# The first chunk's first two attention-times-V blocks issued together, and the next chunk's normalising at other units

## The chip, the cores and the metric

The kernel runs on one core of a Trainium2 chip, in one launch. The metric is the device time of an execution in microseconds (us), the median of several executions. Before the change it is 556.62 us, the median of 3 runs (556.55 to 556.70).

## The reference, cut to what matters

Everything is bfloat16; S = 2048 positions, D = 576, F = 4608, 32 heads of 18.

```python
xn  = layernorm(x)                                  # rows of 576
q, k, v = split(xn @ wqkv)                          # 32 heads of 18
s   = where(0 <= i - j < 256, q k^T / sqrt(18), -1e9)
att = softmax(s) @ v                                # then @ wo
out = x + att @ wo + (silu(xn @ w1) * (xn @ w3)) @ w2
```

## The kernel before, in words

**Tiling.** The 2048 positions are cut into four chunks of 512 (`NC`, `CH`); a chunk is four x tiles of 128 rows. Each chunk has three stages: the projections for q, k and v; then 36 units, each of which makes 128 of the 4608 columns of the gated hidden layer and leaves them in `hT`; then the second stage, which multiplies `hT` by w2 and the attention's output `oT` by wo and writes the result. For chunk 0 the layernorm of its four x tiles and its projections come before the loop over chunks.

**A unit.** It is 18 matmuls in 9 pairs (`unit_pairs`, L746): every matmul uses 64 rows of the array, and the two of a pair go to the two row halves at once, one into each of two PSUM banks. Then ScalarE (ACT) takes the tanh of one bank (`unit_tanh`, L755), and VectorE (DVE) makes `gs` from that bank (L761) and `hT` from `gs` and the other bank (L764). Only when that second DVE instruction has read its bank may TensorE (PE) write the pair of banks again.

**Banks.** Six of the eight PSUM banks are three pairs (`JOBS`), which `job()` deals out in turn: unit u uses the pair that unit u-3 used. The last two banks (`SC`) hold scores. An attention-times-V block takes pairs from the same turn.

**Attention.** The 32 heads are 8 groups of four. In chunk 0 a group has four score steps, 32 in all. A step is 4 or 6 small matmuls on PE (`scores`, L612), an exponential on ACT (`exps`, L621), and one or two masking multiplications on GpSimd (POOL, `masks`, L649). Blocks `pv(c, j)` (L676) multiply the probabilities of groups 2j and 2j+1 by V: 72 matmuls on a 64x20 tile each in chunk 0, 96 in the later chunks. The first matmul of a block waits for the masks of all its steps, and the first one into each bank waits for that bank's last reader. DVE then transposes the two result banks (`pv_out`, L693) and takes reciprocals (L697); POOL scales (`o_scale`, L702); DVE transposes back (`o_turn`, L709); DMAs pack the result into `oT` (`o_pack`, L734).

**Order.** The program is written out by a planner in one pass, and each engine runs its own part strictly in that order, with semaphores where an operand comes from another engine. Between the pairs of the units the planner places score steps by a counter (`clock`, one per pair): the first when it reaches `START`, later ones spaced so that they end before the chunk's last unit, with `PV_COST` counters set aside for every block to come. `BLOCKS` says which blocks are issued together, `AT` in front of which pair of which unit the first of them goes, and `HOLD` keeps score steps away from that place. In chunk 0 before the change blocks 0, 1 and 2 are issued one by one, each at the end of a unit; in chunks 1 to 3 blocks 0 and 1 go together in front of pair 6, 7 or 8 of unit 18, and two probability buffers serve as room for the two extra transposes. Block 3 comes in the second stage in all chunks.

**The next chunk's normalising.** While a chunk's units run, the x tiles of the next chunk are loaded by SyncE's DMA queue (SP; `load_x`, L298; in chunk 0 at units 11, 13, 15 and 17). At the end of the unit that `near` names for a tile, behind that unit's two DVE instructions, DVE takes the statistics (L388 twice, L391), and POOL the inverse root (L370, L372); at a later named unit DVE applies them (L406 twice), and at another a transposing DMA on SP (L448) sends the result to `xnT`. These DVE instructions stand in the program between the two of that unit and the two of the next.

**SP's queue.** It also issues, in program order, nearly all loads of w1 and w3 (`load_part`, L322, six parts for every four units; the parts are tied to places in PE's program by a semaphore), the moves that spread q and k into their places (L557), wo, some of w2, and the packing. ACT's queue issues most of w2 (L354).

Of the kernel before, what the change touches and what calls it, by code (L numbers as in the profile page):

```python
# [44 lines left out]
class _Prog:  # L45
# [13 lines left out]
    def add(self, eng, fn, r=(), w=(), j=(), dma=None, after=()):  # L59
        deps = []  # L60
        for k in r:
            deps += self.bufs[k].writers
        for k in w:
            g = self.bufs.get(k)
            if g is not None:
                deps += g.ahead(eng)
        for k in j:
            g = self.bufs[k].before
            if g is not None:
                deps += g.ahead(eng)  # L70
        op = _Op(eng, fn, deps + list(after), dma)
        op.after = tuple(after)
        self.n[eng] += 1
        op.pos = self.n[eng]
        if dma is not None:
            self.dma_count[dma] = self.dma_count.get(dma, 0) + 16
            op.cnt = self.dma_count[dma]
        for k in r:
            self.bufs[k].readers.append(op)
        for k in w:  # L80
            self.bufs[k] = _Gen([op], self.bufs.get(k))
        for k in j:
            self.bufs[k].writers.append(op)
        for k in w:
            if self.bufs[k].before is not None:
                self.bufs[k].before.before = None
        self.ops.append(op)
        return op
# [76 lines left out]
def bass_parallel_sum__sliding_block__glu_gated_swiglu__prompt_kernel(  # L165
# [21 lines left out]
    NF = F // 128  # L187
# [10 lines left out]
    with ExitStack() as es:  # L198
# [516 lines left out]
        def pack_moves(j):  # L715
            i = j % NOD
            moves = []
            for q in range(4):
                m = 4 * j + q - 2
                if m >= 0:  # L720
                    t, r0 = 2 * (m // 7), Dh * (m % 7)
                    moves.append((oT[r0:r0 + Dh, t:t + 2, :], od[i][32 * q:32 * q + Dh, :, :]))
                else:
                    moves.append((oT[126:128, 2 * q:2 * q + 2, :], od[i][32 * q:32 * q + 2, :, :]))
            for n in range(4 if j == 0 else 0):
                q, p = divmod(n, 2)
                for par in range(2):
                    r0 = 64 * par + 16 * n
                    moves.append((by_par(oT[r0:r0 + 16, 4, :], par), by_par(od[i][32 * q + 2:32 * q + Dh, p, :], par)))
            return moves  # L730

        def o_pack(j, eng, n0=0, n1=4):
            for n, (dst, src) in list(enumerate(pack_moves(j)))[n0:n1]:
                add(eng, lambda e, dst=dst, src=src: e.dma_start(dst, src),  # L734
                    r=[("od", j % NOD), "oTz"], dma=f"oT{j}", **{"j" if n else "w": [("oT", j)]})
# [272 lines left out]

        add("act", lambda e: e.preload_act_table_set("exp_and_others"))

        PV_COST = 6.6
        BLOCKS = [((0,), (1,), (2,))] + [((0, 1), (2,))] * 3
        PV_AFTER = (20, 18, 18, 18)
        START = (60, 46, 46, 46)
        HOLD = 10
        AT = ((NF, 0), (18, 6), (18, 7), (18, 8))
        main, rest = span_main, span_last
        late_spans = {0: [(main, 2, 5, 0, 1, "act")], 1: [(main, 2, 5, 1, 2, "act"), (main, 2, 5, 2, 5, "sp")],
                      **{u: [(rest, 2, 5, u - 2, u - 1, "act")] for u in (2, 3, 4)},
# [3 lines left out]
        for c in range(NC):  # L1023
            NS = len(steps_of(c))
            att = [(g, s) for g in range(G) for s in range(NS)]
            near = {0: (2, 3, 4), 1: (4, 5, 6), 2: (7, 8, 9), 3: (9, 10, 12)}
            if c == 0:
                near = {0: (20, 22, 23), 1: (24, 26, 27), 2: (30, 32, 33), 3: (33, 35, 40)}
            plan = near if c + 1 < NC else {}
            stat, apply, xt = ({v[k]: i for i, v in plan.items()} for k in range(3))  # L1030
            loads = {2: (2,), 5: (3,)} if c + 1 < NC else {}
            if c == 0:
                loads = {11: (0,), 13: (1,), 15: (2,), 17: (3,)}
            total = 9 * NF + len(att) + 3 * PV_COST
            if c:
                total += 9 * sum(COST[kind] for kind, _ in PROJ)
            start = START[c]
            last = total - (18 if c else 12)
            nxt = soon = start
            clock = 0.0  # L1040
# [7 lines left out]
            next_pv = 0  # L1048
            turned = {}

            def later(u, what):
                side.setdefault(u, []).append(what)
# [6 lines left out]
            def score_step():  # L1059
                nonlocal done  # L1060
                g, s = att[done]
                scores(c, g, s)
                exps(c, g, s, take(done))
                masks(c, g, s)
                done += 1
                for i, pairs in enumerate(BLOCKS[c]):
                    if done == 2 * NS * (pairs[-1] + 1):
                        pv_ready[i] = clock + (36 if c and i else PV_AFTER[c])

            def spaced_step():  # L1070
                nonlocal nxt, soon, clock
                score_step()
                soon = clock + 7.5
                room = last - clock - PV_COST * sum(map(len, BLOCKS[c][next_pv:])) - 5 * sum(v > at_u for v in xt)
                nxt = max(soon, clock + room / max(1, len(att) - done))
                clock += 1

            def pv_block(u, mid=False):
                nonlocal next_pv, clock, free, job_ctr, nxt, soon
                block = BLOCKS[c][next_pv]  # L1080
                assert u > turned.get(c, -1) + 1, (c, u, turned)
                next_pv += 1
                pairs = [job() for _ in block]
                for j, banks in zip(block, pairs):
                    pv(c, j, banks)
                clock += PV_COST * len(block)
                if len(block) == 2:
                    nxt, soon = max(nxt, clock + 17), max(soon, clock + 17)
                groups = range(2 * block[0], 2 * block[-1] + 2)
                was = [pt_of[(c, g, s)] for g in groups for s in range(NS)]  # L1090
                assert all(NF - 2 * NHP + 2 * n > u for kind, n in was if kind == "h"), (c, u)
                was = [sl for sl in was if sl[0] != "h"]
                lent = [n for kind, n in was if kind == "pt"][-2:] if len(block) == 2 else []
                free += [sl for sl in was if sl not in [("pt", n) for n in lent]] + [("pt", n) for n in lent]

                def drain(pairs=pairs, lent=lent):
                    borrow(lent)
                    for i in range(2 * len(pairs)):
                        pv_out(pairs[i // 2][i % 2], i)
                    for i in range(2 * len(pairs)):  # L1100
                        o_recip(i)
                    o_scale(0)

                drain() if mid else later(u, drain)
                job_ctr += mid
                k = 0
                for i, g in enumerate(groups):
                    for half in range(2):
                        k += 1 if (i, half) not in ((0, 1), (2, 1)) else 0
                        later(u + k, lambda g=g, half=half: o_turn(g, half))  # L1110
                    if i + 1 < len(groups):
                        later(u + k, lambda i=i: o_scale(i + 1))
                turned[c] = u + k
                for i, j in enumerate(block):
                    later(u + (4 + 3 * i if c else 5), lambda j=j: o_pack(j, "sp"))
                    for n in range(4, 12, 2 if c else 1) if j == 0 else ():
                        later(u + n // 2 + 3 if c else u + n + 1,
                              lambda n=n: o_pack(0, "sp", n, n + 2) if c else o_pack(0, "act", n, n + 1))

            at_u = -1  # L1120
            if c:
# [16 lines left out]
            for u in range(NF):  # L1138
                at_u = u
# [6 lines left out]
                for n in range(9):  # L1146
                    into = nxt - (clock + 9 - n)
                    ahead = 9 * (AT[c][0] - u) + AT[c][1] - n
                    still = next_pv == 0 and 0 <= ahead < HOLD
                    if not still and done < len(att) and (done < len(early) or free) and (clock >= nxt or (n == 8 and into < 3 and clock >= soon)):  # L1150
                        spaced_step()
                    if next_pv == 0 and AT[c] == (u, n):
                        pv_block(u, True)
# [5 lines left out]
                if u % 4 == 3 and u < NF - 8 and (c or u != 15):  # L1159
                    owed += 6  # L1160
                if next_pv in pv_ready and clock >= pv_ready[next_pv] and (next_pv or not AT[c][1]):
                    pv_block(u)
# [22 lines left out]
                if c == 0 and u == 18:  # L1185
                    rows = A_wo[0:4 * Dh, :].rearrange("(n d) f -> n d f", d=Dh)
                    add("sp", lambda e: e.dma_start(wo[126:128, 0:4, :], rows[:, 0:2, :].rearrange("n d f -> d n f")),
                        j=["wo"], dma="wo")
                    for p in range(2):
                        add("sp", lambda e, p=p: e.dma_start(wo[64 * p:64 * p + 64, 4, :], rows[:, 2:Dh, :]),  # L1190
                            j=["wo"], dma="wo")
                if c == 0 and u in (20, 22, 24, 26):
                    load_w2(0, (u - 20) // 2, "act" if u < 24 else "sp")
                if u == 31:
                    xs = [load_x(c * TB + tt) for tt in range(TB)]
            assert done == len(att) and next_pv == len(BLOCKS[c]), (done, next_pv)
            ACC[:] = [[*JOBS[job_ctr % 3], *SC], [*jobs[NF - 2], *jobs[NF - 1]]]
# [7 lines left out]
            n = -3  # L1205
# [62 lines left out]
```

## Time and profile before

| | |
|---|---|
| median of 3 runs | 556.62 us |
| the profiled execution's own time | 556.76 us |
| its span, from first to last instruction | 554.9 us |
| PE busy | 550.5 us, 99% of the span, 8022 matmuls |
| DVE, ACT, POOL busy | 56%, 47%, 38% |
| L746, the units' matmuls (two groups) | 191.5 and 158.5 us busy |
| L817, the second stage's matmuls with w2 | 143.9 us busy |
| L676, the attention-times-V blocks | 15 groups by shape and source, 1.0 to 11.7 us busy each |
| granted PE clock | 1.00 in every stretch |

The profile is of one execution. Its times count from the first instruction; a row of the timeline merges instructions of one line and kind that follow one another and has start, duration, engine, line, operation, what is written and read, the shape and the count; brackets behind it give the engine's idle time before and what ended it. The ends of matmuls are modelled, so the distance from one start to the next is the safer reading. A row with a q behind the engine's name (SPq, ACTq) is the issue of a DMA by that engine's queue, not its transfer.

### The profile page before, as it was taken

To read this page: it belongs to the slowest core of one execution; us is meant where nothing else is said; L and a number is where in the kernel's file an instruction comes from. 1 tells how busy PE (TensorE), PEld (TensorE's weight loads), DVE (VectorE), ACT (ScalarE), POOL (GpSimd) and SP (SyncE) were. 2 spreads that over 40 slices of the span, in tenths; PEclk is the share of its full clock that TensorE was granted. 3 is DMA by queue.
4 is the path that set the end of the run, shared out by engine and by line. 5 is a ranking of instruction groups with operands and counts; after the bars stand their busy time and mean duration, and the time that the engine had idled before them with its cause. 6 is when DMAs were issued, how large, how long until landed. Compare 5 with 4: busy or idle time off the path is not lost.

```text
span 554.9 us, 18260 instructions
## 1 busy us (share of the span) xinstructions
PE 550.5 (99%) x8022; PEld 367.4 (66%) x8022; DVE 313.4 (56%) x587; ACT 260.4 (47%) x365; POOL 210.4 (38%) x380
## 2 busy tenths in 40 slices
PE   8999999999999999999999999999999999999998
PEld 4555545677688854577766665457777666755776
DVE  8466798620469787731057878673105566867211
ACT  7456776100287748610047765860005776686000
POOL 5324576400046537630005653762001554565000
PEclk9999999999999999999999999999999999999999
DMA  9997898568567954656846796356683683632660
GB/s 254 207 195 171 189 225 210 144 178 186 140 141 151 200 130 104 160 141 179 201 109 139 168 190 145 100 141 161 167 200 83 137 176 111 151 103 58 169 163 22
DMA packets 128038, 86.00 MB, mean 155 GB/s; under 512 B 35702, under 2 KB 125646, under 8 KB 127958
## 3 DMA queue, kind: packets, MB, share of 16 engines
q1 hardware_dynamic: 89138, 62.80, 50.4%
q10 hardware_dynamic: 38820, 22.02, 15.7%
q8 instruction: 63, 1.03, 0.8%
q14 instruction: 17, 0.14, 0.1%
HBM read 71.29 MB, written 2.36 MB: 133 GB/s over the span
## 4 chain that ended last, share of the span: by engine, by line
PE 98%; DMA 0%; ACT 0%; DVE 0%; issue 0%
PE ps L746 51%; PE ps L817 29%; PE ps L492 10%; PE ps L612 5%; PE ps L676 3%; DMA xp<-in_A_x_dram 0%; DVE stats L388 0%; ACT hT L382 0%; PE ps L421 0%; ACT sd L361 0%; DVE ofin L839 0%; ACT xnT L434 0%; DVE mv L391 0%
## 5 line engine op out<-in xcount | busy, mean ns | idle before, releaser
L746 PE MATMUL ps<-xnT,w 64*128 64x512 bf16 x1400 | 191.5, 376 | 0.0
L746 PE MATMUL ps<-xnS,w 64*128 64x512 bf16 x1120 | 158.5, 376 | 0.0
L817 PE MATMUL ps<-w,hT 64*128 64x288 bf16 x2292 | 143.9, 282 | 0.0
L761 DVE SCALAR_TENSOR_TENSOR gs<-th,ps 128x512 bf16<-128x512 bf16 x144 | 97.8, 679 | 73.5 <-ACT th L755 72.7
L817 PEld LDWEIGHTS ps<-w,hT 64*128 64x128 bf16 x2292 | 111.9, 94 | 29.7 <-issue 0.8
L746 PEld LDWEIGHTS ps<-xnT,w 64*128 64x128 bf16 x1400 | 84.3, 94 | 50.1 <-DVE ofin L693 0.3
L649 POOL TENSOR_TENSOR pt<-pt,mk 128x256 bf16<-128x256 bf16 (+1 forms) x164 | 98.2, 624 | 27.2 <-ACT pt L621 26.8
L755 ACT ACTIVATE th<-ps 128x512 bf16<-128x512 f32 x144 | 85.6, 595 | 45.7 <-PE ps L746 45.1
L621 ACT ACTIVATE pt<-ps 128x1024 bf16<-128x1024 f32 (+1 forms) x92 | 93.0, 1011 | 29.7 <-PE ps L612 29.0
L764 DVE SCALAR_TENSOR_TENSOR hT<-gs,ps 128x512 bf16<-128x512 bf16 x144 | 98.9, 687 | 5.0
L746 PEld LDWEIGHTS ps<-xnS,w 64*128 64x128 bf16 x1120 | 67.1, 94 | 40.1 <-issue 0.4
L649 POOL TENSOR_TENSOR hT<-hT,mk 128x256 bf16<-128x256 bf16 (+1 forms) x52 | 30.3, 604 | 155.9 <-ACT hT L621 155.9
L505 ACT ACTIVATE stage<-ps 128x512 bf16<-128x512 f32 x16 | 9.6, 597 | 142.7 <-PE ps L492 140.4
L848 DVE TENSOR_TENSOR ofin<-ps,xp 128x288 bf16<-128x288 f32 x31 | 12.2, 450 | 89.0 <-PE ps L817 89.0
L612 PE MATMUL ps<-qv,kv 64*128 64x320 bf16 (+4 forms) x528 | 56.8, 260 | 0.0
L612 PEld LDWEIGHTS ps<-qv,kv 64*128 64x128 bf16 x528 | 31.4, 94 | 21.5 <-ACT pt L621 1.0
L621 ACT ACTIVATE stage<-ps 128x1024 bf16<-128x1024 f32 (+1 forms) x32 | 32.3, 1010 | 15.3 <-PE ps L612 13.5
L492 PE MATMUL ps<-xnT,wp 64*128 64x512 bf16 (+1 forms) x360 | 39.0, 355 | 0.0
L649 POOL TENSOR_TENSOR stage<-stage,mk 128x256 bf16<-128x256 bf16 (+1 forms) x56 | 31.6, 586 | 16.6 <-ACT stage L621 16.6
L621 ACT ACTIVATE hT<-ps 128x1024 bf16<-128x1024 f32 (+1 forms) x28 | 28.4, 1015 | 9.8 <-PE ps L612 9.7
L702 POOL TENSOR_TENSOR oq<-uq,rden 128x288 bf16<-128x288 f32 x13 | 8.7, 673 | 59.8 <-DVE rden L697 59.8
L492 PEld LDWEIGHTS ps<-xnT,wp 64*128 64x128 bf16 x360 | 20.5, 94 | 12.6 <-ACT va L541 0.4
(76 smaller groups left out, 368.0 us busy)
## 6 DMA issues: line engine op xcount, KB each, us to landing
w<-in_B_w_dram SPq DMA_DIRECT2D x210, 192.0 KB, 4.7
w<-in_B_w_dram ACTq DMA_DIRECT2D x70, 288.0 KB, 3.5
xp<-in_A_x_dram SPq DMA_DIRECT2D x29, 144.0 KB, 3.7
out_dram<-ofin SPq DMA_DIRECT2D x31, 72.0 KB, 3.0
xnS<-xnT SPq DMA_DIRECT2D x8, 256.0 KB, 4.9
oT<-od SPq DMA_DIRECT2D x56, 36.0 KB
pt<-in_A_wqkv_dram SPq DMA_DIRECT2D x4, 288.0 KB, 5.1
hT<-in_B_w_dram SPq DMA_DIRECT2D x6, 192.0 KB, 6.8
```

Of the source, the lines that this page charges most:

```text
L492: op = add("pe", lambda e, out_=out_, st=st, mv=mv, n=n, r0=r0, first=first: e.matmul(out_, st, mv, start=first, stop=(part == 1 and n == ...
L505: add("act", lambda e: e.activation(stage[:, t1, :], PS[:, b + 1, :], ACT.Copy), r=[("ps", b + 1)], w=st_keys(t1))
L612: add("pe", lambda e, r0=r0, out_=out_, kb=kb, q0=q0, nb=nb: e.matmul(out_, kb4[r0:r0 + 64, g, kb + NV - NB, :] if kb < 0 else kv[r0:r0 + ...
L621: add("act", lambda e: e.activation(pt_slot(sl)[:, :, 0:w], PS[:, SC[0]:SC[1] + 1, 0:w], ACT.Exp, scale=scale), r=[("ps", b) for b in SC], ...
L649: add("pool", lambda e, vb=vb, mm=mm: e.tensor_tensor(vb, vb, mm, ALU.mult), r=(key if n == 0 else []) + ["mk"], **{"w" if n == 0 else "j" ...
L676: add("pe", lambda e, p=p, q=q, pr=pr, sl=sl, g=g, pos=pos, q0=q0, nb=nb, col=col, first=first, n=n: e.matmul(PS[32 * q:32 * q + VW, banks ...
L746: op = add("pe", lambda e, n=n, r0=r0, r=r, k=k, src=src: e.matmul(PS[:, b0 + r, :], wt[r0:r0 + 64, k, fl * 128:(fl + 1) * 128], src, star ...
L755: add("act", lambda e: e.activation(th[i][:], PS[:, bg, :], ACT.Tanh, scale=0.5), r=[("ps", bg)], w=[("th", i)])
L761: add("dve", lambda e: e.scalar_tensor_tensor(out=gs[i][:], in0=th[i][:], scalar=1.0, in1=PS[:, bg, :], op0=ALU.add, op1=ALU.mult), r=[("t ...
L764: add("dve", lambda e: e.scalar_tensor_tensor(out=hT[:, u, :], in0=gs[i][:], scalar=0.5, in1=PS[:, bu, :], op0=ALU.mult, op1=ALU.mult), r= ...
L817: op = add("pe", lambda e: e.matmul(PS[:, bank, 0:w], stat, move, start=new, stop=False, skip_group_check=True, **tile), r=keys, after=hel ...
L848: add("dve", lambda e: e.tensor_tensor(ofin[:, o, :], PS[:, bank, 0:HD], xp[xs[n]][:, d0:d0 + HD], ALU.add), r=[("ps", bank), ("xp", xs[n] ...
```

## The change

In chunk 0, blocks 0 and 1 are now issued together in front of pair 6 of unit 20, as in the later chunks, and block 2 alone. The score steps of chunk 0 start at counter 50 instead of 60. The statistics, application and sending of the next chunk's four x tiles move from units (20, 22, 23), (24, 26, 27), (30, 32, 33), (33, 35, 40) to (15, 17, 18), (17, 18, 19), (27, 28, 29), (33, 35, 40). A block counts 4.8 in chunk 0 and 6.2 elsewhere, instead of 6.6. Eight packing DMAs of block 0 that ACT's queue issued one by one move to SP's queue, in pairs.

```diff
-        PV_COST = 6.6
-        BLOCKS = [((0,), (1,), (2,))] + [((0, 1), (2,))] * 3
+        PV_COST = (4.8, 6.2, 6.2, 6.2)
+        BLOCKS = [((0, 1), (2,))] * 4
         PV_AFTER = (20, 18, 18, 18)
-        START = (60, 46, 46, 46)
+        START = (50, 46, 46, 46)
         HOLD = 10
-        AT = ((NF, 0), (18, 6), (18, 7), (18, 8))
+        AT = ((20, 6), (18, 6), (18, 7), (18, 8))
...
             if c == 0:
-                near = {0: (20, 22, 23), 1: (24, 26, 27), 2: (30, 32, 33), 3: (33, 35, 40)}
+                near = {0: (15, 17, 18), 1: (17, 18, 19), 2: (27, 28, 29), 3: (33, 35, 40)}
...
             if c == 0:
                 loads = {11: (0,), 13: (1,), 15: (2,), 17: (3,)}
-            total = 9 * NF + len(att) + 3 * PV_COST
+            total = 9 * NF + len(att) + 3 * PV_COST[c]
...
-                room = last - clock - PV_COST * sum(map(len, BLOCKS[c][next_pv:])) - 5 * sum(v > at_u for v in xt)
+                room = last - clock - PV_COST[c] * sum(map(len, BLOCKS[c][next_pv:])) - 5 * sum(v > at_u for v in xt)
...
-                clock += PV_COST * len(block)
+                clock += PV_COST[c] * len(block)
...
                 for i, j in enumerate(block):
-                    later(u + (4 + 3 * i if c else 5), lambda j=j: o_pack(j, "sp"))
-                    for n in range(4, 12, 2 if c else 1) if j == 0 else ():
-                        later(u + n // 2 + 3 if c else u + n + 1,
-                              lambda n=n: o_pack(0, "sp", n, n + 2) if c else o_pack(0, "act", n, n + 1))
+                    later(u + 4 + 3 * i, lambda j=j: o_pack(j, "sp"))
+                    for n in range(4, 12, 2) if j == 0 else ():
+                        later(u + n // 2 + 3, lambda n=n: o_pack(0, "sp", n, n + 2))
```

## The prediction

> **What bounds the kernel now.** I read the page first, for which engine the span hangs on, then PE's waits, then the timelines of chunk 0, where the program changes.
>
> ```profile
> PE 550.5 (99%) x8022; PEld 367.4 (66%) x8022; DVE 313.4 (56%) x587; ACT 260.4 (47%) x365; POOL 210.4 (38%) x380
> PE 98%; DMA 0%; ACT 0%; DVE 0%; issue 0%
> ```
>
> ```profile
> PE ps L887 <- DVE oq L882: 1.2, 1, 1.2
> PE ps L421 <- DVE xn L406: 0.5, 1, 0.5
> PE ps L492 <- ACT xnT L434: 0.3, 1, 0.3
> ```
>
> The first line is busy time by engine, the second the chain that ended last. PE is the chain, and all that it waits is 2.0 us, at the start. So a change can save only what PE spends between matmuls, and whatever makes PE wait in the middle adds to the end in full. Since modelled ends hide gaps, I take distances from start to start.
>
> ```profile
> 20.86 0.83 PE L746 MATMUL ps<-xnT,w 64*128 64x512 bf16 x6
> ...
> 51.87 0.40 PE L746 MATMUL ps<-xnT,hT 64*128 64x512 bf16 x2
> ...
> 53.14 0.37 PE L612 MATMUL ps<-qv,kv 64*128 64x320 bf16 x4
> 53.34 0.59 PE L746 MATMUL ps<-xnT,hT 64*128 64x512 bf16 x4
> ...
> 63.85 1.03 PE L746 MATMUL ps<-xnT,w 64*128 64x512 bf16 x8
> ...
> 67.53 0.81 PE L746 MATMUL ps<-xnS,w 64*128 64x512 bf16 x6
> 68.18 0.38 PE L746 MATMUL ps<-xnT,w 64*128 64x512 bf16 x2
> 68.49 0.31 PE L676 MATMUL ps<-pt,va 64*20 64x320 bf16 x4
> ...
> 69.55 0.37 PE L612 MATMUL ps<-qv,kv 64*128 64x320 bf16 x4
> ```
>
> Three pairs take 68.18 - 67.53 = 0.65 us, so a pair takes 0.216 and a unit 1.94; a score step takes 53.34 - 53.14 = 0.20. Unit 0 starts at 20.86. Hence a unit u with s steps before it starts at 20.86 + 1.94 u + 0.20 s if nothing waits, and that is the clock for the rest.
>
> **What it saves.** Blocks 0 and 1 now cost 53.14 - 51.87 - 0.22 = 1.05 and 69.55 - 68.18 - 0.22 = 1.15 us beyond the unit's last pair, 2.20 together. Of it 68.49 - 68.18 - 0.22 = 0.09 is the change of tile size on the way in, so a block alone is 0.96. Chunk 2 has both forms, joined (first row to second) and single (third to fourth):
>
> ```profile
> 332.78 0.31 PE L676 MATMUL ps<-hT,va 64*20 64x320 bf16 x4
> ...
> 335.12 0.39 PE L746 MATMUL ps<-xnS,w 64*128 64x512 bf16 x2
> ```
>
> ```profile
> 361.88 0.52 PE L676 MATMUL ps<-pt,va 64*20 64x320 bf16 x32
> ...
> 363.12 0.28 PE L612 MATMUL ps<-qv,kb 64*128 64x256 bf16 x2
> ```
>
> Joined takes 2.34, twice single 2.48: joining saves 0.14. So the pair should cost 0.09 + 2 x 0.96 - 0.14 = 1.87 instead of 2.20, a gain of **0.33**. It includes the 0.10 by which the second block's exit is longer than the first's (it waited for the exponential below). The gain lies wholly on PE's chain.
>
> **What it moves onto the path.** Now the normalising. In the changed program's order DVE meets the statistics of x tile 0 right behind unit 15's two instructions, those of tile 1 and the application of tile 0 behind unit 17's, the application of tile 1 behind unit 18's. Before, the first of these stood behind unit 20's. The loads were not moved. The view of the x tile's instructions, for the first and the second of these loads alone, tells when they land:
>
> ```profile
> L298 SPq DMA_DIRECT2D xp<-in_A_x_dram x1: 602/602/602, 53.5 to 53.5; - x1
> DMA to landing us min/median/max: 6.2/6.2/6.2
> ```
>
> ```profile
> L298 SPq DMA_DIRECT2D xp<-in_A_x_dram x1: 1644/1644/1644, 55.5 to 55.5; - x1
> DMA to landing us min/median/max: 6.7/6.7/6.7
> ```
>
> Tile 0 lands at 53.5 + 6.2 = **59.7**, tile 1 at 62.2. SP gets to these issues late because it still has earlier transfers to issue, and nothing ahead of them in its queue is changed. When does DVE want tile 0?
>
> ```profile
> 64.90 0.69 DVE L761 SCALAR_TENSOR_TENSOR gs<-th,ps 128x512 bf16<-128x512 bf16 x1 [0.72 <-ACT th L755]
> 65.63 0.69 DVE L764 SCALAR_TENSOR_TENSOR hT<-gs,ps 128x512 bf16<-128x512 bf16 x1
> ...
> 75.32 0.95 DVE L406 TENSOR_SCALAR xn<-xp,mv,rstd 128x512 bf16<-128x512 bf16 x2
> 76.19 0.67 DVE L761 SCALAR_TENSOR_TENSOR gs<-th,ps 128x512 bf16<-128x512 bf16 x1
> ...
> 79.52 0.78 DVE L388 BATCH_NORM_STATS2 stats<-xp 128x6 f32<-128x288 bf16 x2
> ...
> 80.45 0.63 DVE L761 SCALAR_TENSOR_TENSOR gs<-th,ps 128x512 bf16<-128x512 bf16 x1
> 81.12 0.69 DVE L764 SCALAR_TENSOR_TENSOR hT<-gs,ps 128x512 bf16<-128x512 bf16 x1
> 81.73 0.68 DVE L761 SCALAR_TENSOR_TENSOR gs<-th,ps 128x512 bf16<-128x512 bf16 x1
> ...
> 83.05 1.21 DVE L406 TENSOR_SCALAR xn<-xp,mv,rstd 128x512 bf16<-128x512 bf16 x2
> 84.18 0.67 DVE L761 SCALAR_TENSOR_TENSOR gs<-th,ps 128x512 bf16<-128x512 bf16 x1
> ```
>
> The 63.85 row holds unit 19's last pair, so unit 20 starts at 64.07, and the second row here, unit 19's `hT`, ends at 66.32: 2.25 after the next unit's start. In the changed order unit 16 starts at 20.86 + 16 x 1.94 + 12 x 0.20 = 54.3, and DVE is through with unit 15 near 56.6. So it stands 3.1 us before tile 0's landing, and everything behind it, units 16 to 19, is queued there. From 59.7 DVE works without a pause, priced by these rows: statistics 80.45 - 79.52 = 0.93; a unit with its tanh ready 81.73 - 80.45 = 1.28, its `hT` ending 0.67 + 0.69 = 1.36 after the unit's `gs` starts; an application 76.19 - 75.32 = 0.87 or 84.18 - 83.05 = 1.13.
>
> ```profile
> 8.18 0.58 DVE L406 TENSOR_SCALAR xn<-xp,mv,rstd 128x512 bf16<-128x512 bf16 x2
> ```
>
> ```profile
> 80.62 0.22 POOL L370 TENSOR_SCALAR vpe<-mv 128x1 f32<-128x1 f32 x1 [2.14 <-DVE mv L391]
> 80.93 0.57 POOL L372 TENSOR_TENSOR rstd<-vpe,neghalf 128x1 f32<-128x1 f32 x1
> 81.47 2.74 POOL L649 TENSOR_TENSOR pt<-pt,mk 128x256 bf16<-128x256 bf16 x5
> ```
>
> ```profile
> 68.47 1.02 ACT L621 ACTIVATE stage<-ps 128x1024 bf16<-128x1024 f32 x1 [1.43 <-PE ps L746]
> ```
>
> The application that took 1.13 fell on POOL's masks (81.47 to 84.21); early in the kernel, with POOL idle, one took 0.58. In the changed order POOL too waits for tile 0's statistics (its inverse root stands before the masks of steps 13 to 16) and afterwards works off those masks beside the first application, so I take 1.0 for that one and 0.87 for the second, and keep 0.58 and 1.13 as ends. The Trainium skill, SBUF — State Buffer, section Who interferes with whom, has a rule for it: a VectorE instruction in a two-port mode and GpSimd exclude each other for a whole instruction. The rows agree in sign. By the rule the second application, met by the last mask alone, would cost 0.58 if that mask is over and at most 0.58 + 2.74 / 5 = 1.13 if it has just begun; the sum would come out 0.3 lower or higher than by my 0.87. The root itself takes 80.93 + 0.57 - 80.62 = 0.88; behind tile 0's and six masks of 0.55 tile 1's is ready near 60.7 + 0.9 + 3.3 + 0.9 = 65.8, before DVE asks for it below. For the step from a release to PE's start: the exponential here ended at 69.49 and the score step at 69.55 was behind it, so 0.06.
>
> Step by step: unit 16's `gs` at 59.7 + 0.9 = 60.7, its `hT` ends 62.0. Unit 19 uses unit 16's banks and should start at 20.86 + 19 x 1.94 + 16 x 0.20 = 61.0: **PE waits 1.1**. Unit 17 on DVE until 63.2, statistics of tile 1 (landed) until 64.2, application until 65.2. Unit 18's `hT` ends 66.5; block 0 wants those banks, and PE, now at unit 20's pair 6 at 62.1 + 1.94 + 6 x 0.216 + 0.09 = 65.4, **waits 1.2** more. DVE is through with unit 18 at 66.4, applies tile 1 until 67.3, and unit 19's `hT` ends 68.7; block 1 wants those banks, block 0 is through at 66.6 + 0.96 - 0.14 = 67.4, and **PE waits 1.3**. Sum 3.6, less 0.33: **+3.3**.
>
> After it nothing new is late. The four transposes follow unit 19 at once, and the first two (block 0's banks, wanted by unit 21) run beside block 1 and the three pairs left of unit 20. Chunk 2 has this order after its joined block, and PE, by its list of waits above, never waited there.
>
> **What costs nothing.** The earlier score steps: the same 32 steps at the same spacing of 7 or 8 pairs, with q and k of their groups moved well before; PE covers them, else one exponential each (1.02). `PV_COST` leaves PE's order of chunks 1 to 3 as it was. On SP the transposing sends of tiles 0 and 1 now stand ahead of the six w1/w3 parts for units 28 to 31, and wait for the applications at 65.2 and 67.3; those parts are tied to PE's units 20 to 22 anyway, the last to pair 8 of unit 22, at 20.86 + 22 x 1.94 + 3.2 + 1.9 + 3.6 + 1.7 = 73.9. With the second x load's 6.7 to land that is 81, and unit 28 comes at 20.86 + 28 x 1.94 + 4.8 + 1.9 + 3.6 = 85.5: cover of 4 us, beyond which PE would wait in full. The eight packing issues leave ACT for SP, behind the w1/w3 parts of units 24 to 26; what they pack is wanted only after unit 35. The first w2 issue on ACT, which held the exponential of the 68.47 row up by 1.43, now falls where no score steps are.
>
> **Rivals.** (1) *The x tile is there in time.* If SP issues it sooner, or it lands as x loads do over the kernel:
>
> ```profile
> xp<-in_A_x_dram SPq DMA_DIRECT2D x29, 144.0 KB, 3.7
> ```
>
> then tile 0 lands at 57.2. DVE then waits for unit 17's tanh, whose `gs` starts 64.90 - 64.07 = 0.83 after unit 18's start (20.86 + 18 x 1.94 + 15 x 0.20 = 58.8), at 59.6 or, behind an exponential, near 60; from there 1.28 + 0.93 + 0.73 + 1.28 + 0.73 + 1.36 end at 66.3 (the applications at 0.73, between 0.58 and 0.87, since POOL has nothing to catch up). Block 1 would have started at 65.1, so 1.2 late, net **+0.9**, 557.5. Against it: all before that load in SP's queue is the same. (2) *It does what it says and PE never waits*, **-0.33**, 556.3, not slower. It decides if unit 19's `hT` ends before block 0 is through, at 62.9 + 1.30 + 0.09 + 0.82 = 65.1. It needs DVE to be free of both applications by then, against the landing row and the order of the program. (3) *The gaps throttle PE.* Its first ten matmuls ran slow:
>
> ```profile
> L887 PE MATMUL ps<-oq 128*128 128x512 bf16 x10 | 3.8, 535 | 1.3 <-DVE oq L882 1.2
> ```
>
> They took 3.8 us where ten at a pair's 0.216 take 2.2: 1.6 more. One such spell after the gaps makes +4.9, 561.5. Against it, the three gaps have 3.2 and 0.8 us of work between them. The Trainium skill, TensorE: Matmul & The Clock Gate, section What's actually happening, asks for a whole idle window of about 3.4 us; by that rule no gap here is enough, and rival 3 gives nothing.
>
> **How the numbers follow.** The profiled execution took 556.76 us (span 554.9 and 1.8 around it), 0.14 over the median of the three runs, so the forecast for the median is 556.62 + 3.3 = **559.9**. Chances: forecast 0.78; rival 1 0.12; rival 2 0.05; rival 3 0.05. The forecast's own bounds: the landing between 0.5 earlier and the second load's 6.7 (+0.5), applications 0.58 to 1.13 each (-0.7 to +0.4): 558.7 to 560.8. The range takes in rival 1 and a little above: **557.3 to 561.0**. About 0.2% (1.1 us) is what a measurement of this kernel can tell from no change. Faster by more than that has no case above and gets 0.02; within it are rival 2 and most of rival 1, 0.14; slower is the rest, 0.84.
>
> **What would show it.** In the new profile: DVE's first L388 of chunk 0's units has an idle time of about 3 us ended by the DMA of xp; PE waits for DVE `hT` L764 three times, about 1 us each, at unit 19's start and in front of the two halves of a run of 144 L676 matmuls; after them chunk by chunk the same distances as before. I am wrong if that L388 doesn't wait (rival 1 or 2), if PE waits for w (SP) or for `pt` (masks), or if pairs take 0.43 after the gaps (rival 3).

## The result, and the profile after

The changed kernel takes **560.43 us** (median of 6 runs, 559.78 to 560.89), the kernel before 556.66 beside it (6 runs, 556.51 to 557.16): a ratio of 1.0066, 95% interval 1.0053 to 1.0079, so 3.8 us slower. The profiled execution of the changed kernel has a span of 558.7 us, 3.8 more than before.

The chain that ended last (shares of the span) and the list of PE's waits (line of the waiting instruction, engine and line waited for; us in total, times, longest), of the changed kernel:

```profile
PE 94%; DVE 2%; DMA 1%; ACT 1%; issue 1%; ACTq 0%; POOL 0%; SPq 0%; DVEq 0%
```

```profile
PE ps L746 <- DVE hT L764: 1.5, 1, 1.5
PE ps L887 <- DVE oq L882: 1.2, 1, 1.2
PE ps L676 <- DVE hT L764: 0.9, 1, 0.9
PE ps L746 <- issue: 0.6, 1, 0.6
PE ps L492 <- ACT xnT L434: 0.2, 1, 0.2
PE ps L676 <- POOL pt L649: 0.2, 1, 0.2
```

The chain is still PE's, but 4% of it has gone to others, and four waits in the list are new: two for `hT`, one of "issue" and one for masks. Each has its place in the timeline. The first is the joined block, PE's rows of its two halves:

```profile
64.38 0.31 PE L676 MATMUL ps<-hT,va 64*20 64x320 bf16 x4
...
66.34 0.31 PE L676 MATMUL ps<-pt,va 64*20 64x320 bf16 x4 [0.94 <-DVE hT L764]
...
67.28 0.61 PE L746 MATMUL ps<-xnS,w 64*128 64x512 bf16 x4
```

The second half starts 1.96 us after the first. It takes 0.94 itself to the next matmul of the unit; of that I take 0.09 for the change of tile size, as in the prediction, so without a wait it would have started 0.85 after the first half, and PE lost 1.11 here. The 0.85 is an estimate: no run shows the two halves without any wait. DVE's rows of the same stretch, and the view of x tile 0's load, say why:

```profile
57.27 0.82 DVE L388 BATCH_NORM_STATS2 stats<-xp 128x6 f32<-128x288 bf16 x2 [0.63 <-DMA xp<-in_A_x_dram]
...
60.12 0.69 DVE L761 SCALAR_TENSOR_TENSOR gs<-th,ps 128x512 bf16<-128x512 bf16 x1 [0.41 <-ACT th L755]
...
61.45 0.81 DVE L388 BATCH_NORM_STATS2 stats<-xp 128x6 f32<-128x288 bf16 x2
...
62.42 0.59 DVE L406 TENSOR_SCALAR xn<-xp,mv,rstd 128x512 bf16<-128x512 bf16 x2
62.92 0.68 DVE L761 SCALAR_TENSOR_TENSOR gs<-th,ps 128x512 bf16<-128x512 bf16 x1
...
64.24 0.63 DVE L406 TENSOR_SCALAR xn<-xp,mv,rstd 128x512 bf16<-128x512 bf16 x2
64.78 0.68 DVE L761 SCALAR_TENSOR_TENSOR gs<-th,ps 128x512 bf16<-128x512 bf16 x1
65.50 0.69 DVE L764 SCALAR_TENSOR_TENSOR hT<-gs,ps 128x512 bf16<-128x512 bf16 x1
```

```profile
L298 SPq DMA_DIRECT2D xp<-in_A_x_dram x1: 603/603/603, 53.1 to 53.1; - x1
DMA to landing us min/median/max: 4.1/4.1/4.1
```

The tile was there at 57.25, not at 59.7, and DVE waited 0.63 for it, which delayed nothing that followed: DVE had caught up by unit 17, where it waited 0.41 for the tanh (the second row). But from 60.12 DVE has no gap: unit 17, tile 1's statistics, tile 0's application, unit 18, tile 1's application, unit 19. Unit 19's `hT` ends at 66.19, and the second half wants its banks.

The second place is the end of chunk 0, DVE's, PE's and SP's rows:

```profile
93.28 0.69 DVE L764 SCALAR_TENSOR_TENSOR hT<-gs,ps 128x512 bf16<-128x512 bf16 x1
97.17 0.77 DVE L709 STREAM_TRANSPOSE od<-oq 128x256 bf16<-128x256 bf16 x2 [3.20 <-DMA oT<-od]
...
98.55 0.69 DVE L764 SCALAR_TENSOR_TENSOR hT<-gs,ps 128x512 bf16<-128x512 bf16 x1
```

```profile
99.29 0.60 PE L746 MATMUL ps<-xnT,w 64*128 64x512 bf16 x4 [1.54 <-DVE hT L764]
```

```profile
88.06 4.37 SPq L734 DMA_DIRECT2D oT<-od  x6
92.47 1.42 SPq L322 DMA_DIRECT2D w<-in_B_w_dram  x2
93.94 1.35 SPq L734 DMA_DIRECT2D oT<-od  x2
```

Block 2's turned result goes into the buffer `od[0]` (there are two, dealt out by block number), out of which block 0's twelve packing DMAs read. SP issued the last two of them at 93.94 to 95.29, behind w1/w3 parts and block 1's packing. DVE stood 3.20 us in front of the turn, with units 31 and 32 queued behind it, and PE stood in front of unit 34. In the kernel before, ACT had issued the last of the eight at 80.7, and DVE turned at 90.9 without a wait:

```profile
80.69 0.59 ACTq L734 DMA_DIRECT2D oT<-od  x1
```

```profile
90.93 0.76 DVE L709 STREAM_TRANSPOSE od<-oq 128x256 bf16<-128x256 bf16 x2
```

The third and fourth are smaller: block 2's first matmul waits for masks, and the first matmul of chunk 1's unit 12 for what the profile can't name ("issue"):

```profile
87.85 0.33 PE L676 MATMUL ps<-pt,va 64*20 64x320 bf16 x8 [0.18 <-POOL pt L649]
```

```profile
184.65 0.61 PE L746 MATMUL ps<-xnT,w 64*128 64x512 bf16 x4 [0.57 <-issue]
```

The starts of the same units in the two traces, compared, show how it adds up. With score steps counted out, the changed kernel is 1.05 later from unit 30 on (the joined block's 1.11 and block 2's 0.25 from single starts, less 0.33 that joining saves), 2.72 at unit 35 (1.70 more at unit 34), 3.26 after chunk 1 (0.77 more at unit 12, 0.20 back at its joined block), 3.81 after 0.24 in chunk 2 and 0.31 in chunk 3.

### The profile page after: what moved, and what is told of

Same layout as the page of the kernel before. It is cut to its first block, busy times and chain, and to the rows that moved or that the text cites. A ratio compares the mean times of both kernels' runs of the same rounds, so it can differ in the third digit from the quotient of the medians.

```text
span 558.7 us, 18260 instructions
## 1 busy us (share of the span) xinstructions
PE 551.7 (99%) x8022; PEld 365.9 (65%) x8022; DVE 312.7 (56%) x587; ACT 260.5 (47%) x365; POOL 210.1 (38%) x380
## 3 DMA queue, kind: packets, MB, share of 16 engines
q8 instruction: 63, 1.03, 0.8%
## 4 chain that ended last, share of the span: by engine, by line
PE 94%; DVE 2%; DMA 1%; ACT 1%; issue 1%; ACTq 0%; POOL 0%; SPq 0%; DVEq 0%
PE ps L746 48%; PE ps L817 29%; PE ps L492 9%; PE ps L612 5%; PE ps L676 3%; DVE hT L764 1%; DVE gs L761 1%; DMA xp<-in_A_x_dram 0%; DMA oT<-od 0%; DVE stats L388 0%; ACTq L557 0%; ACT th L755 0%; ACT stage L505 0%; DVE xn L406 0%; DVE od L709 0%
## 5 line engine op out<-in xcount | busy, mean ns | idle before, releaser
L746 PEld LDWEIGHTS ps<-xnS,w 64*128 64x128 bf16 x1120 | 66.3, 94 | 41.1 <-issue 0.4
L709 DVE STREAM_TRANSPOSE od<-oq 128x256 bf16<-128x256 bf16 x64 | 25.8, 428 | 6.3 <-DMA oT<-od 3.2
```

Of the source, the lines that this page charges most:

```text
L709: add("dve", lambda e: e.transpose(od[i][:, g % 2, c0:c0 + CH // 2], oq[:, c0:c0 + CH // 2]), r=["oq", "oq0"], **{"j" if half or g % 2 els ...
L746: op = add("pe", lambda e, n=n, r0=r0, r=r, k=k, src=src: e.matmul(PS[:, b0 + r, :], wt[r0:r0 + 64, k, fl * 128:(fl + 1) * 128], src, star ...
```

## Experiments

The theory after the result: two costs in chunk 0 that add up, DVE's normalising in front of the joined block's second half (1.1) and the reuse of `od[0]` (1.7); joining by itself saves 0.33 on PE; chunk 1's wait is a third thing. All numbers "over" are medians against the kernel before on the same chip.

| run | over the kernel before, us | ratio (95% interval) |
|---|---|---|
| e1_other_od | +2.58 | 1.0044 (1.0031 to 1.0056) |
| e2_pack_act | +2.30 | 1.0039 (1.0027 to 1.0052) |
| e3_x_late | +9.60 | 1.0171 (1.0157 to 1.0185) |
| e4_both | +2.31 | 1.0036 (1.0022 to 1.0050) |
| e5_before_x | +0.91 | 1.0017 (1.0008 to 1.0026) |
| e6_joined_21 | +2.84 | 1.0053 (1.0040 to 1.0067) |
| e7_x_early | +5.26 | 1.0093 (1.0079 to 1.0107) |
| e8_x_late_od | +3.86 | 1.0066 (1.0053 to 1.0078) |
| e9_three_back | +0.17 | 1.0008 (0.9999 to 1.0016) |
| e10_sp_lighter | +2.13 | 1.0035 (1.0023 to 1.0048) |
| e11_all | +0.34 | 1.0007 (0.9998 to 1.0016) |

**e1: another buffer for block 2.**

```diff
-            i = g // 2 % NOD
+            i = (0, 1, 1, 0)[g // 2]
```

(and the same in `pack_moves` and `o_pack`; the new order holds in all four chunks).

> The changed kernel, but chunk 0's block 2 turns into the buffer that block 1 packed from (od[1], four packing DMAs, landed at 93.0 us in the changed kernel's trace) and not into block 0's (od[0], twelve, landed at 96.6). Nothing moves in any queue. Theory (the turn of block 2 waits for block 0's packing DMAs, now in SP's queue, and costs PE 1.70 at unit 34): DVE's idle time of 3.20 us ended by oT<-od goes, unit 34 starts 1.7 earlier against the kernel before, and the time is 3.8 - 1.7 = 2.1 us over the kernel before. Rival (unit 34 is late because ACT or SP are late with something else in this stretch): still 3.8 over.

In the trace DVE turns at once, as its rows show, and the step at unit 34 is gone; unit 35, counted from unit 0, is 1.66 earlier than in the changed kernel.

```profile
93.20 0.69 DVE L764 SCALAR_TENSOR_TENSOR hT<-gs,ps 128x512 bf16<-128x512 bf16 x1
93.81 0.76 DVE L709 STREAM_TRANSPOSE od<-oq 128x256 bf16<-128x256 bf16 x2
```

That shows the second cost: no queue was moved, only the buffer. In the medians the gain is 1.2, and the two intervals just overlap; the 1.7 is read from the traces. The median is 0.5 higher than expected; the trace's own end is 2.08 later than before, with 1.05 at chunk 1's unit 12, where the changed kernel had 0.77.

**e2: the eight packing DMAs on ACT.**

```diff
-                        later(u + n // 2 + 3, lambda n=n: o_pack(0, "sp", n, n + 2))
+                        later(u + n // 2 + (3 if c else 2),
+                              lambda n=n: o_pack(0, "sp" if c else "act", n, n + 2))
```

> The changed kernel with chunk 0's eight small packing DMAs issued by ACT in units 24 to 27 in place of SP in units 25 to 28. Theory: od[0] is free before block 2, so the 1.70 of unit 34 go; SP is through with chunk 0 some 5 us earlier (8 x 0.65). If chunk 1's +0.55 (a part of w1/w3 that lands late for unit 12) is left over from SP's backlog of chunk 0, it goes as well: +1.5 over the kernel before; if it is not, +2.1. Rival (ACT can't spare 8 x 0.62 us in four units): tanh late in units 24 to 27, PE waits there for DVE hT, and the time stays near +3.8.

The step at unit 34 goes here too, and the one in chunk 1, but the time is +2.30 and not +1.5. PE waited 0.4 for exponentials, and the joined block came later: in this execution tile 0 landed at 58.0 and tile 1 at 62.05, DVE waited for both, and now the first half waits as well.

```profile
58.02 0.82 DVE L388 BATCH_NORM_STATS2 stats<-xp 128x6 f32<-128x288 bf16 x2 [1.43 <-DMA xp<-in_A_x_dram]
...
62.07 0.82 DVE L388 BATCH_NORM_STATS2 stats<-xp 128x6 f32<-128x288 bf16 x2 [0.39 <-DMA xp<-in_A_x_dram]
```

```profile
65.08 0.31 PE L676 MATMUL ps<-hT,va 64*20 64x320 bf16 x4 [0.67 <-DVE hT L764]
```

The second wait is the one that counts: tile 1's statistics start 0.62 later than in the changed kernel (62.07 for 61.45), with no gap on DVE behind them, and the joined block starts 0.70 later (65.08 for 64.38). It is the dependence that the prediction described, met at the other tile.

**e3: the normalising at the units of before.**

```diff
-                near = {0: (15, 17, 18), 1: (17, 18, 19), 2: (27, 28, 29), 3: (33, 35, 40)}
+                near = {0: (20, 22, 23), 1: (24, 26, 27), 2: (30, 32, 33), 3: (33, 35, 40)}
```

> The changed kernel, with the statistics, applications and sends of chunk 0's x tiles at the units of the kernel before (20, 22, 23; 24, 26, 27; 30, 32, 33). Theory (block 1 waits 1.13 because unit 19's two DVE instructions are queued behind the statistics and both applications): block 1 follows block 0 at once, the stall goes, and with the od wait as it is the time is 3.8 - 1.1 = 2.7 over the kernel before. Rival 1 (the four transposes behind the joined block fill DVE, and whatever is queued behind them is late there): PE waits for hT at units 23 to 26 instead, still about +3.8. Rival 2 (block 1 waits for something of its own, masks or banks): the stall stays at block 1.

The total missed by 7 us, and the trace separates the two causes. The halves of the block:

```profile
65.20 0.31 PE L676 MATMUL ps<-hT,va 64*20 64x320 bf16 x4
...
66.26 0.31 PE L676 MATMUL ps<-stage,va 64*20 64x320 bf16 x4
```

The second row is the half's second group of matmuls; its first is merged with the half before it and starts 0.01 earlier. So the halves are 1.05 apart, not 1.96, and until unit 33 the kernel runs 0.12 ahead of before: the first cost is the normalising. Chunk 0's loss is all at units 34 and 35, where the other cost grew: SP now has the send of tile 1 in front of block 0's last two packing DMAs (issued from 97.52), and DVE waits for them.

```profile
100.63 0.77 DVE L709 STREAM_TRANSPOSE od<-oq 128x256 bf16<-128x256 bf16 x2 [6.89 <-DMA oT<-od]
```

Behind that PE ran slow for a unit: unit 34 took 107.46 - 103.68 = 3.78 us instead of some 1.95, the 1.84 lost at unit 35. Two stretches, PE's gap and the unit after it (start and end, length; busy time of PE, PEld, DVE, ACT, POOL with the number of instructions; granted clock, DMA share, GB/s):

```profile
97.00:103.60 6.60, 0.39 (x4) 0.00 (x0) 2.90 (x8) 1.30 (x2) 1.76 (x4) 0.77 0.71 182
103.60:107.40 3.80, 3.72 (x18) 1.32 (x20) 3.73 (x9) 0.00 (x0) 2.61 (x5) 0.50 0.56 163
```

The granted clock is 0.50 in the second: the throttling of the prediction's rival 3, at 1.84 (it had priced a spell at 1.6) for a gap of 6.29. I had taken the `od` wait "as it is" although the edit moves a send within the queue that sets it: the same oversight as in the prediction.

**e4: the edits of e2 and e3 together.**

> Both: x tiles at the units of the kernel before, and the eight packing DMAs on ACT in units 24 to 27. What is left of the change is the joined block with its score steps. Theory (two costs that add up, and a gain of 0.33 by joining): 3.8 - 1.7 - 1.1 = +1.0 if chunks 1 to 3 keep their +0.55, +0.24 and +0.31, and -0.33 if those are left over from chunk 0's backlogs. Rival (joining gains nothing, or another wait comes up): about +1 with a new wait for hT in units 21 to 26.

+2.31 is a miss. Until unit 26 it is within 0.15 of before, then PE's list of waits has a new entry, for score steps whose banks ACT had not yet read:

```profile
PE ps L612 <- ACT pt L621: 1.3, 2, 0.8
```

Two DMA issues a unit on ACT delay the exponentials; the kernel before had one a unit. From the starts of the units, PE is 1.85 later than before at unit 30, and 0.76 more is lost at chunk 1's unit 12.

**e5: the kernel before with the new places of the normalising alone.**

```diff
-                near = {0: (20, 22, 23), 1: (24, 26, 27), 2: (30, 32, 33), 3: (33, 35, 40)}
+                near = {0: (15, 17, 18), 1: (17, 18, 19), 2: (27, 28, 29), 3: (33, 35, 40)}
```

> The kernel before with one edit alone: chunk 0's x tiles normalised and sent at the units of the changed kernel (15, 17, 18; 17, 18, 19; 27, 28, 29). Theory (the early normalising costs PE time only where a block's banks are wanted right behind it): unit 19's second DVE instruction ends near 66.2 again, but here single blocks stand at units 14 and 21 and nothing wants unit 19's banks before unit 22 at 69.7, so the time is that of the kernel before, within 0.3. Rival (the early place costs PE about 1 by itself, DVE being behind): +0.7 to +1.3, with PE waiting for hT near units 19 to 22.

No wait of PE near units 19 to 22 although unit 19's `hT` ended at 68.45 here: early normalising costs nothing where no block stands behind it, as the theory has it. The time is +0.91 all the same, where the expectation allowed 0.3. In the trace 0.81 of it appears at one place, in the middle of unit 30:

```profile
90.36 0.60 PE L746 MATMUL ps<-xnS,w 64*128 64x512 bf16 x4 [0.64 <-issue]
```

No load ended there that the profile shows; what this wait was stays open.

**e6: e1, with the joined block one unit later.**

```diff
-        AT = ((20, 6), (18, 6), (18, 7), (18, 8))
+        AT = ((21, 6), (18, 6), (18, 7), (18, 8))
```

> The changed kernel with block 2 turning into od[1] (as in the run e1) and the joined block one unit later (unit 21, pair 6), the normalising where the change put it. Its second half now wants unit 20's banks, and no statistics or application stands between units 19 and 20 on DVE. Theory: the wait between the halves (1.1 in the changed kernel) shrinks to the 0.2 or less that the run e3 showed with DVE in time, so unit 35 starts 1 us earlier than in e1, level with the kernel before within 0.2; the end is 0 to -0.2 against the kernel before, or +0.5 to +1 if the last w1/w3 part for chunk 1's unit 12 lands late as in e1 (+1.05 there). Rival (the wait belongs to the joined block itself, whatever stands on DVE): 1.1 again, +2.

A miss: one unit is not enough. Tile 1 landed at 62.35 in this execution, DVE was behind by as much as before, and both halves waited. A third wait of 2.02, in unit 23, is again one that the profile doesn't name, and its cause stays open; the profiled execution took 561.03, 1.5 over the median of its runs, so part of it is of that execution alone. The run's rival, that the wait belongs to the joined block itself, is not excluded here; e3 and e9 exclude it.

```profile
67.61 0.31 PE L676 MATMUL ps<-hT,va 64*20 64x320 bf16 x4 [0.79 <-DVE hT L764]
69.02 0.31 PE L676 MATMUL ps<-pt,va 64*20 64x320 bf16 x4 [0.40 <-DVE hT L764]
```

**e7: e1, with the x loads and the normalising of tiles 0 and 1 earlier.**

```diff
-                near = {0: (15, 17, 18), 1: (17, 18, 19), 2: (27, 28, 29), 3: (33, 35, 40)}
+                near = {0: (12, 13, 14), 1: (14, 15, 16), 2: (27, 28, 29), 3: (33, 35, 40)}
...
-                loads = {11: (0,), 13: (1,), 15: (2,), 17: (3,)}
+                loads = {9: (0,), 10: (1,), 15: (2,), 17: (3,)}
```

> The changed kernel with block 2 turning into od[1], and x tiles 0 and 1 loaded at units 9 and 10 (were 11 and 13) and normalised and sent at units 12, 13, 14 and 14, 15, 16. DVE then has nothing but unit 17, 18 and 19's own instructions ahead of the joined block. Theory: the wait between the halves falls from 1.1 to 0.2 or less; end 0 to -0.2 against the kernel before, +0.5 to +1 with a late w1/w3 part in chunk 1. Against it: if the tiles land as late as before (57.2 and later), DVE stands waiting for them from unit 12 or 14 on, and PE loses more than now (+4 or more).

The case against it came true: the load, asked for two units earlier, was issued only at 51.03 (2.1 sooner), and DVE stood before it with units 13 and the next behind; +5.26. The trace is of the fastest of the five executions, 560.58, at a granted clock of 1.00; the other four, 561.49 to 563.09, have a mean of 0.997, so PE was throttled for a while in them. What they waited for, no trace shows.

```profile
53.96 0.82 DVE L388 BATCH_NORM_STATS2 stats<-xp 128x6 f32<-128x288 bf16 x2 [3.50 <-DMA xp<-in_A_x_dram]
```

**e8: the edits of e1 and e3 together.**

> The run e3 (x tiles at the units of the kernel before) with block 2 turning into od[1]. In e3 block 0's last two packing DMAs stood on SP behind the send of x tile 1 and landed at 100.1, block 1's four at 95.3, and DVE wanted to turn at 93.7. Theory: DVE's wait falls from 6.9 to about 1.6, which PE's spare of about 1.7 behind a unit just hides or nearly so: unit 35 within 0.5 of the kernel before, where e3 was 8.2 late; end +0 to +1.3 (chunk 1's late part included). Rival (e3's loss is of another kind, w1/w3 parts behind the sends): stays several us late.

DVE's wait fell to 2.42, not 1.6; that is over PE's spare, and unit 34 waited 1.8. With these edits SP's queue bounds that place, whichever of the two buffers is wanted.

```profile
95.48 0.77 DVE L709 STREAM_TRANSPOSE od<-oq 128x256 bf16<-128x256 bf16 x2 [2.42 <-DMA oT<-od]
```

**e9: e8, with the eight packing DMAs on ACT, one a unit as before.**

```diff
-                    for n in range(4, 12, 2) if j == 0 else ():
-                        later(u + n // 2 + 3, lambda n=n: o_pack(0, "sp", n, n + 2))
+                    for n in range(4, 12, 2 if c else 1) if j == 0 else ():
+                        later(u + n // 2 + 3 if c else u + n + 1,
+                              lambda n=n: o_pack(0, "sp", n, n + 2) if c else o_pack(0, "act", n, n + 1))
```

> The changed kernel with three things put otherwise: x tiles at the units of the kernel before (as in e3), block 2 turning into od[1] (as in e1), and the eight small packing DMAs on ACT again, one a unit (units 25 to 32). Of the change stay the joined block and its score steps. In e8, SP got to block 1's packing DMAs 3.3 us late for DVE with the eight still ahead of them; without their 8 x 0.65 us it should be in time. In e4, ACT with two of them a unit made PE wait 1.3 for exponentials; one a unit was free in the kernel before. Theory (the two costs and nothing else in chunk 0): unit 35 level with e3 before its stall, that is 0.1 earlier than the kernel before; the end -0.1, or +0.6 to +0.9 if chunk 1's w1/w3 part is late again. Rival (joining costs by itself): +1 or more with waits for ACT or DVE in units 21 to 33.

PE's waits, and the block's two halves:

```profile
PE ps L887 <- DVE oq L882: 1.2, 1, 1.2
PE ps L492 <- ACT xnT L434: 0.2, 1, 0.2
PE ps L676 <- issue: 0.2, 1, 0.2
```

```profile
64.51 0.31 PE L676 MATMUL ps<-hT,va 64*20 64x320 bf16 x4
...
65.57 0.31 PE L676 MATMUL ps<-stage,va 64*20 64x320 bf16 x4
```

The waits for `hT` and for masks and the one in chunk 1 are gone (0.2 of "issue" is new), and the time is that of the kernel before: +0.17, the interval includes 1. So all that the changed kernel loses lies in what was moved around the joined block. Nothing is won either: the halves are 1.05 apart instead of 0.85, because unit 19's `hT` ends 2.4 us after the start of unit 20 and this place wants its banks 0.2 earlier even with DVE free, and of the 0.33 that joining saves 0.02 to 0.12 are left in the traces of e3, e8 and e9. That is below what a measurement of this kernel can tell. In front of chunk 2's joined block the trace of e9 is 0.12 ahead of before, and it loses 0.5 there, where the 0.2 of "issue" stands; the cause stays open.

**e10: e1, with chunks 1's and 2's x loads of units 2 and 5 issued by ACT.**

```diff
-                        xslot[(c + 1) * TB + i] = load_x((c + 1) * TB + i)
+                        xslot[(c + 1) * TB + i] = load_x((c + 1) * TB + i, "act" if c else "sp")
```

> The run e1 with one edit: in chunks 1 and 2 ACT issues the two x loads of units 2 and 5 in place of SP, which takes 0.47 + 0.58 us of issues out of SP's queue ahead of the last w1/w3 part for unit 12. In e1 that part was issued 21.8 us after chunk 1's start and landed at 27.13, PE wanted it at 26.18 and waited 1.05; in the runs where it was issued by 21.0 it landed by 25.15 and PE did not wait. Theory (SP's queue is behind there): it is issued by 20.8, lands before 26.2, the step at chunk 1's unit 12 goes, and the end is 2.6 - 1.0 = +1.6 over the kernel before. Rival (the part is late by its own transfer, or the step is the fetch of something else): the step stays, +2.6.

In the trace the step at chunk 1's unit 12 is gone and the end is 1.09 later than before, 0.98 less than in e1; the part was issued 21.1 us after the chunk's start (20.8 expected, 21.8 in e1). The median, +2.13, is only 0.45 below that of e1 and the intervals overlap, so it is the trace that shows it, not the time; and the trace is of the fastest of the five executions (557.77, the others 558.18 to 558.87), so for those it isn't shown. The landing moved by more than the issue. The views of the last two w1/w3 parts for unit 12, in the changed kernel, the kernel before and e10; the very last part is the upper end of the first row, the lower of the second and the upper of the third:

```profile
DMA to landing us min/median/max: 3.8/4.5/5.2
```

```profile
DMA to landing us min/median/max: 4.2/4.2/4.3
```

```profile
DMA to landing us min/median/max: 3.7/3.8/3.8
```

The same part took 5.2 us where PE waited and 4.2 or 3.8 where it did not; the last section comes back to that.

**e11: e9 and e10 together.**

> Both edits, e9 and e10 together. Theory: the joined block with neither of the three waits: -0.1 to -0.3 against the kernel before. Rival (what is lost in chunk 1 belongs to the joined kernel in any form): +0.5 to +1.

+0.34, the interval includes 1: again the kernel before, within what can be told. No version beat it.

## Why the prediction was right, and where it was not

- **The bound: right.** PE's chain carries the time, and waits in the middle add in full: the four new ones of the list, with the smaller steps in the later chunks and less what joining saves, make up the 3.8.
- **What joining saves, 0.33: right as PE's own work, but no run had it.** In single starts the pair takes 1.86 less its wait, against 1.87 forecast; but that rests on the estimated 0.85. Where the normalising was out of the way, in e3, e8 and e9, the second half still waited 0.2, and at most 0.12 was won.
- **"Tile 0 lands at 53.5 + 6.2 = 59.7": wrong, and with it two of the three waits.** The issue came when expected (53.13); the transfer took 4.1. So the 1.1 at unit 19's start and the 1.2 in front of block 0 did not come. I had taken one transfer of one execution for a property of the load. What happened at this place is rival 1, which had 0.12: it had the landing at 57.2 (57.25 measured), block 1's start at 66.3 (66.34) and its wait at 1.2 (1.11). By the prediction's own signs its forecast was wrong here: DVE's first L388 waited 0.63 and not about 3, and PE waited for masks and, as the landings tell, for a w1/w3 part. e2, where the tiles landed later, and e3, where the normalising was moved away, show the dependence from both sides.
- **The price of the applications: too high.** From one's start to the next instruction 62.92 - 62.42 = 0.50 and 64.78 - 64.24 = 0.54, forecast 1.0 and 0.87. POOL's rows:

```profile
61.53 1.05 POOL L649 TENSOR_TENSOR stage<-stage,mk 128x256 bf16<-128x256 bf16 x2
...
63.48 0.67 POOL L649 TENSOR_TENSOR stage<-stage,mk 128x256 bf16<-128x256 bf16 x1
```

  The masks end at 62.58 and 64.15, so the first application met 0.16 of one and the second none. The Trainium skill, SBUF — State Buffer, section Who interferes with whom, has DVE in a two-port mode and GpSimd exclude each other; the trace agrees in that the application that no mask met cost 0.54, near the 0.58 that the rule gave in the prediction, while 1.13 was paid beside masks.
- **"The eight packing issues leave ACT for SP [...] what they pack is wanted only after unit 35": the step that failed.** What they write is wanted late, what they read from is wanted early: the next block but one needs `od[0]`. I priced a moved DMA by its consumer and not by the release of its source. It cost 1.70 in the traces, nearly half of the result, as e1 shows.
- **"After it nothing new is late", and equal distances in chunks 1 to 3: wrong** by 0.25 at block 2 (masks), 0.77 at chunk 1's unit 12 and 0.55 in chunks 2 and 3. SP reached that w1/w3 part 179.35 - 175.57 = 3.78 later than before, where PE was 2.72 later, and the part took 1.0 longer. The cover before was 181.19 - 179.78 = 1.41: 3.78 + 1.0 - 2.72 - 1.41 = 0.65, near the 0.57 of PE's row.
- **Rival 3, throttling: did not happen.** The row of the stretch with the joined block (columns as in e3):

```profile
62.00:70.00 8.00, 7.06 (x194) 3.94 (x191) 7.86 (x20) 1.20 (x3) 2.73 (x6) 1.00 1.25 172
```

  The granted clock stays 1.00, in the stretches behind it too: gaps of 0.9 and 1.5 us don't throttle, the 6.29 of e3 did. The Trainium skill, TensorE: Matmul & The Clock Gate, section What's actually happening, puts the point between them, at a whole idle window of about 3.4 us; the traces agree. No run here has a gap of that length, but e3's rows allow an estimate: a mean of 0.77 over 97.00 to 103.60, if the clock went from 1.00 to 0.50 once, puts the fall near 100.6, about 3.2 us into the gap.

The sum of 3.3 stood near the 3.8 because waits of 2.3 that did not come were replaced by 3.0 that I had priced at nothing (1.70, 0.25, 0.54 in chunk 1 and 0.55 behind it). That the sum came so near is luck: the time lay in the range, but of the forecast's mechanism only the wait in front of block 1 happened, and that as a rival had it.

## What to carry to other kernels

When a DMA is moved to another queue, ask two questions: who wants what it writes, and who wants to overwrite what it reads; the second is easily missed, and an engine that runs in order stops with everything behind it. Before putting work of an in-order engine ahead of a block, count from the block back: its banks are free only when the last user's whole queue is through. And a transfer time read once is one draw, not a price: look for the same load elsewhere in the trace before building three waits on it.

## What the hardware showed that I had not expected

A load's time jumped by 1 to 2 us when a block of PE's own instructions was fetched during it. The traces list instruction fetches as DMA queues of their own; q8 has 63 of 16 KB, 1.03 MB in all, which I take for PE's, since for its 8022 matmuls and 8022 weight loads that is 64 bytes each. From the issue of the last part for chunk 1's unit 12 to 0.1 us before its landing in the kernel before (175.57 to 179.67), and for 4.55 us from its issue in the changed kernel (179.35 to 183.90), the queue rows (packets, MB, share of 16 engines) are:

```profile
q1 hardware_dynamic: 1445, 0.90, 113.8%
```

```profile
q8 instruction: 1, 0.02, 1.7%
```

In the first window q1, the loads, is the only queue; in the second q8 has one packet. Over all 13 traces it divides without exception: in the seven where PE waited at that place, a fetch began 2.2 to 2.8 us before the part landed (182.33 for 184.56 in the changed kernel), and the part took 5.0 to 5.6 us; in the six where PE did not wait, a fetch began at most 0.12 before the landing, if at all, and the part took 3.8 to 4.2. The first two x tiles that chunk 0 loads have the same pattern: in the kernel before, a fetch began at 55.42, between tile 0's issue and its landing, and it took 6.2; in the changed kernel the next one came at 59.49, after both tiles, and they took 4.1 and 4.4; in e2 at 58.63, and tile 1 took 6.2. For tiles 0 and 1 the other traces fit too: 6.1 to 6.7 us where a fetch began 3 to 7 us before the landing, 2.9 to 5.1 where none did so or it began at most 1.5 before it. But a fetch isn't all that makes a load long: tile 2 in the changed kernel, issued at 61.67, took 6.4 with no fetch in flight. That the fetch causes the delay is argued from these, not tested by itself. It would explain why moving a few instructions of PE changes the time of loads that were not touched, and why the load times of before did not hold after.
